# Linear attention with a feed-forward layer: other durations in the planner, and an order number of its own for every unit and step

## The chip, the cores and the metric

The kernel runs on one core of a Trainium2 chip. The metric is the device time of one execution in microseconds. Three runs of the kernel before the change took 551.27, 548.26 and 547.93 us; the median is 548.26 us.

## The reference

There are 4 batches, 8 heads, 768 positions and 48 values per head. An attention with a decaying state per head is followed by a feed-forward layer of width 2048 with squared ReLU over all 3072 tokens, in float32.

```python
for t in range(S):
    kt, vt, rt, wt = (k[:, :, t], v[:, :, t], r[:, :, t], w[:, :, t])
    cur = np.einsum('bhd,bhe->bhde', u[None] * kt, vt)
    y[:, :, t] = np.einsum('bhd,bhde->bhe', rt, state + cur)
    state = wt[:, :, :, None] * state + np.einsum('bhd,bhe->bhde', kt, vt)
x = np.ascontiguousarray(y.transpose(0, 2, 1, 3)).reshape(B * S, H * D)
h = np.maximum(x @ w_in, 0.0)
return h * h @ w_out
```

## The kernel before

The sequence is cut into 6 chunks of 128 positions. A chunk of one batch is a unit (24 units). For a unit, `attention(c, b, rank)` issues these steps: loads of r, k, w (`load`, two batches at a time) and of v (`v`); in chunk 0 transposes on TensorE (`turn`, L479), later a block transpose on DVE (`z`, L442) with 16 small transfers that spread it (`pt`, L452); the running products of the decay on DVE (`scan`, L491); their inverse through logarithm and exponential on ACT (`ln`, L498 and L499); scaled receptances (`rt`, L502) and keys (`kn`, L508, L509, L514) on DVE; the products with u on POOL (`rk`, L521 and L523) and their sums on DVE (`beta`, L527 to L530); the diagonals of the score matrices on ACT (`diag`, L541); a test of the value range on ACT (`far`, L543 and L544); the scores on TensorE (`mt`, L554); masks on DVE (`mask`, L557); then on TensorE the product with the state and the transposed keys (`ktp`, L576 and L581), after a copy on ACT (`kt`, L600) the product with the values and the outer product for the new state (`mix`, L589 and L608; in chunk 0 with a selection product L616 and a copy L620); the result x in a high and a low part on ACT and DVE (`x` and `x3`, L650 and L651), part of it moved by transfers (`send`, L658); and the state update on DVE and POOL (`S`, L670 and L673).

The feed-forward layer takes the 2048 hidden values in 16 blocks of 128, for each chunk. `ffn` issues per block nine hidden products (`hp`, L693) into one of two PSUM banks, the squared ReLU and its split in a high and a low part (`g`, L698 to L702, alternately ACT and DVE, three buffers), and per batch three output products (`ob`, L708) that add up in one of four banks. After the last block the banks are copied and stored (`os`, L715 to L719). The first 6 blocks of chunk 0 and all 16 of chunk 1 are done in two halves of two batches (256 columns instead of 512). The weights come in 8 groups (`load_w`), each split into a high and a low part on ACT, DVE and POOL (`split_w`, L393 to L414).

No instruction is issued by `attention` or `ffn` directly. Each call of `P.add` records a step with its engine, a planned duration, an order number (`rank`), and what it reads and writes. `Plan.order` then plays the whole program through with these durations: of the steps whose inputs are there, an engine takes the one that can start first, and among those the one with the lowest number. In the resulting order the instructions are emitted, so every engine has a fixed queue. The planned durations, the delays between engines (`LAT`), the queue times of transfers (`QUEUES`, `START`, `SLACK`) and the time to change TensorE between the whole array and its parts (`SWITCH`) act only through this order. In the first 110 us by the planner's own clock, it also fills gaps that it foresees on TensorE with throw-away transposes (fillers, L749): the gap less 0.3 us, divided by 0.12 us. The class `Ranks` gives the order numbers by formulas: an offset per step name, and per chunk, batch, weight group or feed-forward block a base.

[...]

## Time and profile before

| | |
|---|---|
| median of the runs | 548.26 us |
| span of the profiled execution | 546.8 us |
| matmul busy (PE) | 525.6 us, 96% |
| DVE, ACT, POOL busy | 368.9, 284.4, 101.8 us |
| idle time on PE, from the start to the first hidden product at 42.70 us | 7.66 us |
| from there to the first full-width hidden product at 83.20 us | 3.15 us |
| from there to the last matmul at 540.30 us | 3.92 us |
| the end, after it | 6.50 us |

The profile gives for the profiled execution its span, from the first to the last instruction, and no other time of it. PE is TensorE's matmuls, PEld its weight loads, DVE VectorE, ACT ScalarE, POOL GpSimd, SP the queue that issues most transfers. A row of the timeline has start and length in us, engine, line, operation, output and inputs, the number of instructions, and in brackets the idle time of the engine just before, with what ended it.

### The profile page before, as it was taken

How to read it: one execution, taken by the hardware profiler on the slowest of the kernel's cores; microseconds unless marked ns; L12 is line 12 of the kernel's file. 1: busy time of each engine (PE TensorE's matmuls, PEld its weight loads, DVE VectorE, ACT ScalarE, POOL GpSimd, SP SyncE). 2: the span in 40 equal slices, each digit the busy share in tenths (PEclk: the TensorE clock that was granted, in tenths of full speed). 3: DMA queues.
4: the chain of work that ended last, by engine and by line, in shares of the span. 5: the costliest groups of instructions: out<-in, count | busy, mean ns of one | idle time of the engine just before them, and what ended most of it. 6: DMA issues, size and time to landing. Idle time of an engine off the chain costs nothing.

```text
span 546.8 us, 12903 instructions
## 1 busy us (share of the span) xinstructions
PE 525.6 (96%) x5033; PEld 465.9 (85%) x5033; DVE 368.9 (67%) x770; ACT 284.4 (52%) x730; POOL 101.8 (19%) x121
## 2 busy tenths in 40 slices
PE   7889899999999998999999999999999999999995
PEld 6778798888899988988788887988888998998995
DVE  6979988998869676978869686886543423423322
ACT  3858586576664837475464747455343322432322
POOL 5234545152303102031303021020000000000000
PEclk9989999999999998999999999999999999999999
DMA  9989969447566575656546646633001000010001
GB/s 161 195 227 239 230 131 253 74 69 137 105 115 120 92 148 97 127 99 121 107 83 118 123 82 129 148 68 65 1 16 63 11 1 2 21 38 0 1 0 63
DMA packets 222979, 53.02 MB, mean 97 GB/s; under 512 B 212672, under 2 KB 217792, under 8 KB 222912
## 3 DMA queue, kind: packets, MB, share of 16 engines
q1 hardware_dynamic: 220016, 50.75, 46.7%
q10 hardware_dynamic: 2896, 1.38, 1.1%
q8 instruction: 42, 0.69, 0.6%
q14 instruction: 25, 0.20, 0.1%
HBM read 31.65 MB, written 4.72 MB: 67 GB/s over the span
## 4 chain that ended last, share of the span: by engine, by line
PE 40%; DVE 6%; SPq 2%; issue 1%; DMA 1%; ACT 1%; ACTq 0%; DVEq 0%
PE ob L708 19%; PE hp L693 18%; SPq L452 2%; DVE st L442 1%; PE a L589 1%; PE a L576 1%; DMA st<-in_r_dram 1%; DVE m L557 1%; PE a L554 1%; DVE pt L514 1%; DVE g L702 1%; DVE pt L491 0%; DVE m L509 0%; DMA v<-in_v_dram 0%; DVE pt L508 0%
## 5 line engine op out<-in xcount | busy, mean ns | idle before, releaser
L708 PE MATMUL ob<-wo,g 128*128 128x384 f32 x1152 | 224.0, 341 | 0.0
L693 PE MATMUL hp<-x,wi 128*128 128x512 f32 (+1 forms) x1062 | 220.0, 355 | 1.1 <-DVE g L702 1.0
L708 PEld LDWEIGHTS ob<-wo,g 128*128 128x128 f32 x1152 | 198.8, 188 | 5.2 <-issue 0.5
L693 PEld LDWEIGHTS hp<-x,wi 128*128 128x128 f32 x1062 | 175.2, 189 | 28.9 <-DVE g L702 2.8
L699 DVE SCALAR_TENSOR_TENSOR hp<-hp,t 128x512 f32<-128x512 f32 (+1 forms) x118 | 70.1, 594 | 83.4 <-ACT t L698 82.5
L698 ACT ACTIVATE t<-hp 128x512 f32<-128x512 f32 (+1 forms) x118 | 61.1, 518 | 107.3 <-PE ob L708 87.2
L702 DVE TENSOR_TENSOR g<-hp,g 128x512 fp32r<-128x512 f32 (+1 forms) x118 | 68.8, 583 | 34.7 <-ACT g L701 34.0
L701 ACT CAST g<-hp 128x512 fp32r<-128x512 f32 (+1 forms) x118 | 59.6, 505 | 58.2 <-DVE hp L699 58.1
L541 ACT ACTIVATE m<-diag,beta 128x64 f32<-128x64 f32 x192 | 50.7, 342 | 25.1 <-DVE beta L529 23.5
L521 POOL TENSOR_TENSOR st<-st 128x384 f32<-128x384 f32 x24 | 25.7, 1071 | 62.7 <-DVE st L442 60.6
L491 DVE TENSOR_TENSOR_SCAN pt<-pt,zero 112x128 f32<-112x128 f32 x80 | 30.1, 411 | 0.3 <-DMA pt<-st 0.2
L442 DVE STREAM_TRANSPOSE st<-st 128x1152 f32<-128x1152 f32 x20 | 27.2, 1363 | 4.2 <-DMA st<-in_r_dram 4.2
L554 PEld LDWEIGHTS a<-pt 48*64 48x64 f32 x768 | 19.1, 134 | 11.4 <-issue 3.2
L651 DVE SCALAR_TENSOR_TENSOR x<-a,x 112x128 fp32r<-112x128 f32 (+2 forms) x68 | 20.4, 329 | 11.2 <-ACT x L650 10.9
L557 DVE COPY_PREDICATED m<-caus,a 128x384 f32<-128x384 uint8 x48 | 26.3, 582 | 1.8 <-PE a L554 1.6
L554 PE MATMUL a<-pt 48*64 48x128 f32 (+1 forms) x768 | 22.6, 252 | 5.0 <-DVE pt L514 3.1
L589 PEld LDWEIGHTS a<-m,v 64*48 64x48 f32 (+1 forms) x768 | 20.2, 127 | 7.3 <-issue 3.2
L650 ACT ACTIVATE x<-a 112x128 fp32r<-112x128 f32 (+2 forms) x68 | 18.2, 316 | 15.6 <-PE a L608 7.6
L523 POOL TENSOR_TENSOR st<-st,un 128x384 f32<-128x384 f32 x24 | 24.9, 1040 | 1.4
L589 PE MATMUL a<-m,v 64*48 64x64 f32 (+3 forms) x768 | 24.3, 250 | 0.6 <-ACT nothing L640 0.5
L673 POOL TENSOR_TENSOR S<-S,Ec 112x192 f32<-112x192 f32 x16 | 9.4, 589 | 76.0 <-DVE S L670 71.2
L498 ACT ACTIVATE m<-pt 112x512 f32<-112x512 f32 x24 | 15.1, 633 | 15.5 <-DVE pt L491 15.3
(86 smaller groups left out, 441.7 us busy)
## 6 DMA issues: line engine op xcount, KB each, us to landing
pt<-st SPq DMA_DIRECT2D x120, 96.0 KB, 2.3
ro<-in_moe_w_out_dram SPq DMA_DIRECT2D x8, 768.0 KB, 6.9
v<-in_v_dram SPq DMA_DIRECT2D x88, 48.0 KB, 2.5
st<-in_w_dram SPq DMA_DIRECT2D x11, 384.0 KB, 4.0
st<-in_k_dram SPq DMA_DIRECT2D x11, 384.0 KB, 5.1
st<-in_r_dram SPq DMA_DIRECT2D x11, 384.0 KB, 6.1
out_dram<-q SPq DMA_DIRECT2D x20, 192.0 KB, 1.9
ri<-in_moe_w_in_dram SPq DMA_DIRECT2D x8, 384.0 KB, 6.5
```

Of the source, the lines that this page charges most:

```text
L442: V.transpose(out=zt[:, i].rearrange("a t p q i -> a t (p q) i"), in_=sv[:, :, i].rearrange("s t p q x -> s t (p q) x"))
L491: lambda p=p: V.tensor_tensor_scan(out=pt[:, 0, p], data0=src(0)[:, p], data1=zero.broadcast_to([HP, C]), initial=1.0, op0=ALU.mult, op1=A ...
L541: A.activation(Ms[j].tile[:, mo(p, y):mo(p, y) + Q], diag2, AF.Copy, scale=beta.tile[:, i:i + 1])
L554: T.matmul(mts[j].tile[q * Q:q * Q + Q, o:o + C - y * Q], kq[js, g:g + Q], pt[js, 1, 2 * q + p, y * Q:], start=True, stop=True, skip_group ...
L557: P.add("dve", 0.53, rank("mask"), lambda j=j: V.copy_predicated(out=mv(Ms[j]), mask=caus.broadcast_to([128, 2, W]), data=mv(mts[j])), r=[ ...
L589: T.matmul(spot(p)[to:to + n + D, y * Q:], vt.tile[qs, o - n:o + D], Ms[j].tile[qs, mo(p, y):mo(p, y) + C - y * Q], start=(c == 0 and p == ...
L693: T.matmul(hp.tile[:, 0:n], wi[f][:, wl, kt], xT[:, kt, xl, xs], start=(m == 0), stop=(m == 3 * KT - 1))
L698: P.add("act", 0.5 if full else 0.28, rank("g"), lambda: A.activation(t(), h(), AF.Relu), r=[hp], w=[(g, 1)])
L699: P.add("dve", 0.61 if full else 0.33, rank("g"), lambda: V.scalar_tensor_tensor(out=h(), in0=h(), scalar=0.0, in1=t(), op0=ALU.max, op1=A ...
L701: P.add("act", 0.53 if full else 0.31, rank("g"), lambda: A.copy(out=hi(), in_=h()), r=[hp], w=[(g, 0)])
L702: P.add("dve", 0.61 if full else 0.33, rank("g"), lambda: V.tensor_tensor(out=lo(), in0=h(), in1=hi().bitcast(F32), op=ALU.subtract), r=[h ...
L708: T.matmul(obs[b][:, 0:DM], g.tile[0][:, gl, o:o + C], wo[f][:, wl], start=(f == 0 and m == 0), stop=(f == NF - 1 and m == 2))
```

## The change

The planner gets other figures throughout: delays between engines, the first transfer's delay (`START` 2.4 to 3.6), the margin after a transfer (`SLACK` 2.0 to 1.0), three times instead of one for changing TensorE's mode, an issue time for each transfer instead of one per queue, and other durations for nearly all steps. [...] The tiles for v are taken in unit order from chunk 1 on. The order numbers come from tables: one per unit and step name (`UNITS`, 24 rows of 23), one per weight group (`LOAD`, `SPLIT`), one per feed-forward block and step name (`FFN`). What is computed, and with which instructions, stays; the number of fillers goes from 169 to 183. All line numbers behind the class `Ranks` grow by 139.

```diff
-    LAT = {"pe": 0.24, "act": 0.14, "dve": 0.14, "pool": 0.15}
-    QUEUES = {"sp": 0.5, "actq": 0.36}
-    LANES, RUNS, SLACK, START = 8, 2300, 2.0, 2.4
-    SWITCH, KEEP = 0.094, 1.0
+    LAT = {"pe": 0.22, "act": 0.13, "dve": 0.11, "pool": 0.13}
+    QUEUES = ("sp", "actq")
+    LANES, RUNS, SLACK, START = 8, 2300, 1.0, 3.6
+    ENTER, LEAVE, BETWEEN, KEEP = 0.147, 0.2, 0.09, 1.0
...
-                free[unit] = at + self.QUEUES[s.engine]
+                free[unit] = at + s.issue
...
-                        free[unit] += self.SWITCH
+                        free[unit] += self.ENTER if not mode else self.BETWEEN if s.mode else self.LEAVE
...
-    U0 = (-83, -59.75, 60, 76.25)
-    OFF = {'hp': 147.75, 'g': 6.75, 'ob': 70, 'os': 85.75}
-    LAG = 80
+    UNITS = (
+        (-1354.91, -1161.61, 40.98, -392.53, -1448.01, 172.35, -3.19, -1499.94, -1249.87, 191.9, -1500, 1014.93, -6.91, -1480, 150.66, 35.23, 145.22, -1468.33, 0, 0, 0, 0, 0),
...
+    FFN = {
+        (0, 1.0): (1232.86, 185.26, -86.32, 0),
...
-        return 32 * (c - 1) + 8 * b - 4 + self.AT[name]
+        return self.UNITS[4 * c + b][self.NAMES.index(name)]
...
-        vt = Slot("v" if c else "v0")
+        vt = Slot("v", 4 * c + b) if c else Slot("v0")
...
-                P.add("pe", 0.5, rank("turn"), turn, r=[(st, ui, i)], w=[ps[i]])
+                P.add("pe", 0.36, rank("turn"), turn, r=[(st, ui, i)], w=[ps[i]])
...
-        P.add("dve", 0.75, rank("beta"), sums, r=[(st, ui, 1)], w=[beta])
+        P.add("dve", 1.04, rank("beta"), sums, r=[(st, ui, 1)], w=[beta], port=True)
...
-        P.add("pe", 0.95, rank("mt"), scores, r=RK + KK, w=mts, mode=1, claim=Ms)
+        P.add("pe", 0.69, rank("mt"), scores, r=RK + KK, w=mts, mode=1, claim=Ms)
...
-            P.add("dve", 0.53, rank("mask"), lambda j=j: V.copy_predicated(out=mv(Ms[j]), mask=caus.broadcast_to([128, 2, W]), data=mv(mts[j])), r=[mts[j]], w=[Ms[j]])
+            P.add("dve", 0.47, rank("mask"), lambda j=j: V.copy_predicated(out=mv(Ms[j]), mask=caus.broadcast_to([128, 2, W]), data=mv(mts[j])), r=[mts[j]], w=[Ms[j]])
...
-        P.add("pe", 2.1 if full else 1.1, rank("hp"), first, r=wkeys("wi") + [x for b in range(*bs) for x in xkeys(c, b)], w=[hp])
+        P.add("pe", 2.075 if full else 1.07, rank("hp"), first, r=wkeys("wi") + [x for b in range(*bs) for x in xkeys(c, b)], w=[hp])
...
-            P.add("pe", 0.525, rank("ob"), second, r=wkeys("wo") + [(g, 0), (g, 1)], w=[("ob", b)])
+            P.add("pe", 0.52, rank("ob"), second, r=wkeys("wo") + [(g, 0), (g, 1)], w=[("ob", b)])
```

Three places of the order show what moves. The first is ACT's queue in chunk 0, from the step that begins the split of the second group of `w_out` (`ro_62`) to the x of the second unit (`x_136`); `m` with `diag` are diagonals, `m_158<-a` the copies of the second unit's transposed keys. Before:

```order
L393 ACTIVATE q_150<-ro_62 128x768
L541 ACTIVATE m_159<-diag_125,beta_170 128x64 x4
L600 COPY m_158<-a_147 128x224
L600 COPY m_158<-a_148 128x224
L541 ACTIVATE m_161<-diag_125,beta_170 128x64 x4
L541 ACTIVATE m_160<-diag_125,beta_171 128x64 x4
L466 DMA v_94<-in_v_dram 64x4x48 x2
L650 ACTIVATE x_136<-a_147 128x2x128
L650 ACTIVATE x_136<-a_148 128x128
```

And now:

```order
L532 ACTIVATE q_150<-ro_62 128x768
L680 ACTIVATE m_159<-diag_125,beta_171 128x64 x4
L680 ACTIVATE m_161<-diag_125,beta_171 128x64 x4
L789 ACTIVATE x_136<-a_147 128x2x128
L789 ACTIVATE x_136<-a_148 128x128
L739 COPY m_158<-a_147 128x224
L739 COPY m_158<-a_148 128x224
```

The x of the second unit stands after two groups of diagonals instead of three, and ahead of the copies instead of behind them.

The second is DVE's queue where the last two units of chunk 0 get their keys: `pt_130<-a` (L514, now L653) is the key product that the scores of such a unit wait for, `beta` are the sums of a unit of chunk 1 (before), `S` is a state update, `hp` and `g` belong to the feed-forward layer. Before:

```order
L670 TENSOR_TENSOR S_133<-a_148,Ec_166 112x96
L527 TENSOR_REDUCE beta_168<-st_151 128x8
L528 TENSOR_TENSOR beta_168<-beta_168 64x4
L529 TENSOR_TENSOR beta_168<-beta_168 64x4
L530 TENSOR_TENSOR beta_168<-beta_168 64x4
L514 TENSOR_TENSOR pt_130<-a_147,m_157 112x2x4x64
L702 TENSOR_TENSOR g_97<-hp_146,g_97 128x256
```

And now, around both key products of this pair:

```order
L809 TENSOR_TENSOR S_132<-a_148,Ec_165 112x96
L648 SCALAR_TENSOR_TENSOR m_156<-pt_130,m_156 112x512
L653 TENSOR_TENSOR pt_130<-a_147,m_157 112x2x4x64
L838 SCALAR_TENSOR_TENSOR hp_146<-hp_146,t_96 128x256
L653 TENSOR_TENSOR pt_130<-a_148,m_156 112x2x4x64
L841 TENSOR_TENSOR g_95<-hp_146,g_95 128x256
```

The sums of the unit of chunk 1 (L527 to L530) stand directly ahead of a key product before; now none do.

The third is TensorE's queue in chunk 1, at the unit of batch 0 (state `S_131`): the last scores (`a<-pt`, L554, now L693) and the first products with the state (L576, now L715). Before:

```order
L554 MATMUL a_148<-pt_129 64x64
L708 MATMUL ob_142<-wo_71,g_97 128x384 x3
L693 MATMUL hp_145<-x_136,wi_77 128x512 x9
L576 MATMUL a_147<-pt_129,S_131 64x128
L576 MATMUL a_147<-pt_129,S_131 48x128
```

And now:

```order
L693 MATMUL a_147<-pt_129 64x64
L693 MATMUL a_148<-pt_129 64x64
L715 MATMUL a_147<-pt_129,S_131 64x128
L715 MATMUL a_147<-pt_129,S_131 48x128
L715 MATMUL a_148<-pt_129,S_131 48x128
```

An output and a hidden product stood between the scores and the state product of this unit; now nothing does.

More of the change, by code (lines that the diff above doesn't have):

```diff
@@ L55, in pool, with add @@
         self.pools[name] = [[0.0, t] for t in tiles]
-    def add(self, engine, cost, rank, fn, r=(), w=(), after=(), runs=128, port=False, mode=0, claim=(), more=0):
+    def add(self, engine, cost, rank, fn, r=(), w=(), after=(), runs=128, port=False, mode=0, claim=(), more=0, issue=0.5):
         s = Step()
+        s.issue = issue
         s.mode, s.more, s.fill = mode, more, (0, None)
@@ L196 @@
-    AT1 = {'load': -67.5, 'z': 222.75, 'pt': -247.25, 'rk': 205.25, 'beta': 122.75, 'far': 121, 'v': -0.25, 'scan': 54, 'ln': 129.25, 'rt': -164.5, 'kn': -179, 'diag': 307, 'mt': -111.75, 'mask': -258.5, 'ktp': -150.5, 'kt': -29, 'mix': -182.5, 'x': 282, 'x3': -277.75, 'send': -154.5, 'dS': 325, 'S': -15.75}
-    U0 = (-83, -59.75, 60, 76.25)
-    C1 = (-17.75, 54, 74.25, 163.25)
-    W0 = (-263.75, -87.25, -59.25, -20.75, 22.25, 4.5, 110.5, 165.5)
-    WL = (-93.5, -123, -116.25, -63, -46.75, -41.25, -197.5, -176.25)
@@ L201 @@
-    OFF = {'hp': 147.75, 'g': 6.75, 'ob': 70, 'os': 85.75}
-    LAG = 80
-    def unit(self, c, b, name):
-        if c == 0:
-            return self.U0[b] + self.AT0[name]
-        if c == 1:
-            return self.C1[b] + self.AT1[name]
-        return 32 * (c - 1) + 8 * b - 4 + self.AT[name]
+    NAMES = ('load', 'v', 'turn', 'scan', 'ln', 'rt', 'kn', 'rk', 'beta', 'diag', 'far', 'mt', 'mask', 'mix', 'kt', 'x', 'dS', 'S', 'z', 'pt', 'ktp', 'x3', 'send')
+    UNITS = (
[24 rows of a table added]
+    )
+    LOAD = (-1273.71, -900.27, -547.16, -422.59, 579.46, 579.24, 858.31, 1017.12)
@@ L379, in load_w @@
             n = (2 * R, D, D, D, D)[i]
-            P.add("sp", 0.0059 * n if i < KT else 0.5, rank, lambda to=to, src=src: nc.sync.dma_start(out=to, in_=src),
-                  w=[("wi", g, i)], after=before, runs=n)
-        P.add("sp", 2.4, rank, lambda: nc.sync.dma_start(out=wo_r[g], in_=w_out32[g]), w=[("wo", g, 0, 0)],
-              after=before, runs=256)
+            P.add("sp", (1.45, 0.72, 0.72, 0.47, 0.47)[i], rank, lambda to=to, src=src: nc.sync.dma_start(out=to, in_=src),
+                  w=[("wi", g, i)], after=before, runs=n, issue=0.48)
+        P.add("sp", 2.7, rank, lambda: nc.sync.dma_start(out=wo_r[g], in_=w_out32[g]), w=[("wo", g, 0, 0)],
+              after=before, runs=256, issue=0.5)
     def split_w(g, rank):
@@ L434, in load @@
                                           in_=src[b0:b0 + m, :, ss, :].rearrange("b h s d -> s (b h) d"))
-                    P.add("sp", 1.05 * m, rank("load") + b0 - b, load, w=[(st, x, i) for x in range(b0 - b, b0 - b + m)], after=after, runs=128 * H * m)
+                    P.add("sp", 0.25 + 0.94 * m, rank("load") + b0 - b, load, w=[(st, x, i) for x in range(b0 - b, b0 - b + m)], after=after, runs=128 * H * m, issue=0.6)
             if c > 0:
@@ L599, in evacuate @@
             for i, t in enumerate(both_yb):
-                P.add("act", 0.3, rank("kt"), lambda i=i, t=t: A.copy(out=kv(Kt, i * 2 * HP, None), in_=kv(t, 2 * C, None)), r=[(t, "kt")], w=[(Kt, i)])
+                P.add("act", 0.24, rank("kt"), lambda i=i, t=t: A.copy(out=kv(Kt, i * 2 * HP, None), in_=kv(t, 2 * C, None)), r=[(t, "kt")], w=[(Kt, i)])
         def outer():
```

220 lines of the change are left out of this document (169 added, 51 removed), and 23 rows, old and new, of the table UNITS.

## The prediction

> **What bounds the kernel now.** I read the page first: its busy rows and the chain that ended last say that TensorE (PE) sets the end and that DVE, ACT and POOL do not.
>
> ```profile
> span 546.8 us, 12903 instructions
> PE 525.6 (96%) x5033; PEld 465.9 (85%) x5033; DVE 368.9 (67%) x770; ACT 284.4 (52%) x730; POOL 101.8 (19%) x121
> PE 40%; DVE 6%; SPq 2%; issue 1%; DMA 1%; ACT 1%; ACTq 0%; DVEq 0%
> ```
>
> Then the busy time by stretch, cut where the program changes its kind of work: up to the first hidden-layer product (42.7), to the first full-width one (83.2), through the attention of the later chunks, and the end. Behind the span stand the busy times of PE (x matmuls), the granted PE clock, the DMA share and GB/s.
>
> ```profile
> 0.00:42.70 42.70, 35.04 (x396) 0.96 0.99 194
> 42.70:83.20 40.50, 37.35 (x417) 1.00 0.94 199
> 83.20:180.00 96.80, 96.18 (x1065) 1.00 0.63 125
> 180.00:270.00 90.00, 87.70 (x1083) 0.98 0.59 112
> 270.00:540.30 270.30, 269.30 (x2079) 1.00 0.25 51
> 540.30:546.80 6.50, 0.02 (x1) 0.89 0.35 122
> ```
>
> PE stands idle 42.70 - 35.04 = 7.66 us, then 3.15, 0.62, 2.30 and 1.00: 14.7 us before the last matmul. The 6.50 at the end are the copy and store of the last outputs. The change leaves every matmul of the computation in place, so what it can win is this idle time, slow-clock time, and fillers, the throw-away transposes that the planner puts into gaps it foresees during the first 110 us of its own reckoning. The program has 169 fillers before and 183 after. Where they stand matters more than how many there are.
>
> **The first stretch.** The columns of the next rows are start, length, engine, line, operation, count and, in brackets, idle time before it.
>
> ```profile
> 12.12 2.67 PE L749 MATMUL a<-ident 128*128 128x128 f32 x23
> 36.52 0.93 ACT L393 ACTIVATE q<-ro 128x768 f32<-128x768 f32 x1 [1.69 <-DMA ro<-in_moe_w_out_dram]
> 37.34 0.82 ACT L541 ACTIVATE m<-diag,beta 128x64 f32<-128x64 f32 x3
> 38.30 0.57 ACT L600 COPY m<-a 128x224 f32<-128x224 f32 x2
> 38.76 2.03 ACT L541 ACTIVATE m<-diag,beta 128x64 f32<-128x64 f32 x8
> 40.69 0.54 ACT L650 ACTIVATE x<-a 128x256 fp32r<-128x256 f32 x2
> 37.08 5.07 PE L749 MATMUL hp<-ident 128*128 128x128 f32 x31
> 42.08 0.68 PE L608 MATMUL a<-v,m 64*64 64x48 f32 x32
> 42.69 1.34 PE L693 MATMUL hp<-x,wi 128*128 128x256 f32 x9
> ```
>
> A filler takes 2.67 / 23 = 0.116 us at the full clock. The first hidden product at 42.69 waits for two things: the x of the second unit (batch 1), which ACT writes at 40.69, and the outer product of that unit (L608), which stands ahead of it on PE behind 31 fillers. Both come after ACT's wait for a weight load that lands at 36.52. The order of ACT from that load on is the first place shown with the change: one group of four diagonals (L541) and the issue of two loads leave the way to x, and x moves ahead of the copies. The loads on SP's queue keep their order as far as this weight group, so I keep its landing. After: 36.52 + 0.82 (step to the next) + 1.93 (eight diagonals, 38.76 to 40.69) + 0.54 (x) + 0.57 (copies) = 40.4, outer product 0.61 and a hand-over, first hidden product at 41.4: 1.3 us earlier. Against it stands the first unit. The mask of its second half moves on DVE behind the second unit's key product and sums and two steps of a weight split, the fillers ahead of its first value product grow from 13 to 37 (24 x 0.116 = 2.8 us), and its copies on ACT fall behind the logarithms of the next pair, so PE reaches the second unit's scores some 3 us later. That just about uses up the wait for the load. If it runs over, the cover is gone and the 29 extra fillers ahead of the first hidden product (143 before, 172 after) are paid: 29 x 0.116 = 3.4 us. Bounds -1.3 to +3.4; I take 0, since both chains meet within a microsecond.
>
> **The second stretch (42.7 to 83.2).** PE interleaves the last two units of chunk 0 with half-width hidden products.
>
> ```profile
> 58.48 1.64 DVE L528 TENSOR_TENSOR beta<-beta 64x4 f32<-64x4 f32 x1
> 60.15 0.91 DVE L529 TENSOR_TENSOR beta<-beta 64x4 f32<-64x4 f32 x1
> 61.91 0.90 PE L554 MATMUL a<-pt 48*64 48x128 f32 x32 [2.03 <-DVE pt L514]
> 64.50 0.88 PE L749 MATMUL hp<-ident 128*128 128x128 f32 x6
> 68.84 1.36 PE L749 MATMUL hp<-ident 128*128 128x128 f32 x11
> 73.63 0.82 PE L749 MATMUL a<-ident 128*128 128x128 f32 x6
> ```
>
> The longest stall, 2.03 us, is PE waiting for the last key product (L514) of a unit. That stood on DVE behind the sums of a unit of the next chunk, two of whose tiny steps took 1.64 and 0.91 us. In the new order (second place) both key products of this pair stand close behind one another with no sums ahead of them, so this stall has no cause left. Fillers in this stretch fall from 26 to 11: 15 x 0.116 = 1.7 us. Of the 3.15 us idle I do not take all: each of the three filler groups that remain leaves at least the 0.3 us that the planner's rule subtracts, so 1.1 us in all, and I allow one short stall of 0.74 (the row at 270.33 below): 3.15 - 1.84 = 1.3. Together -3.0, bounds -4.9 (all of it) to 0 (each stall comes back elsewhere).
>
> **The third stretch (83.2 to 540.3).** Three stalls are left here, and one costs more than its length. The last four rows are single microseconds; behind the span: PE, PEld, DVE, ACT and POOL busy (x instructions), then clock, DMA share and GB/s.
>
> ```profile
> 146.97 1.34 PE L693 MATMUL hp<-x,wi 128*128 128x256 f32 x9 [0.54 <-DVE g L702]
> 206.63 1.60 PE L554 MATMUL a<-pt 48*64 48x128 f32 x32 [1.89 <-DVE S L670]
> 270.33 1.03 PE L576 MATMUL a<-pt,S 48*64 48x128 f32 x16 [0.74 <-DVE m L557]
> 207.00:208.00 1.00, 1.00 (x31) 1.00 (x30) 0.97 (x2) 0.00 (x0) 1.00 (x3) 0.69 0.91 156
> 208.00:209.00 1.00, 1.00 (x11) 0.88 (x7) 0.93 (x4) 0.22 (x1) 0.54 (x1) 0.50 0.82 143
> 209.00:210.00 1.00, 1.00 (x6) 1.00 (x5) 1.00 (x3) 1.00 (x5) 0.00 (x0) 0.50 0.72 124
> 210.00:211.00 1.00, 1.00 (x7) 0.99 (x6) 1.00 (x3) 1.00 (x5) 0.00 (x0) 0.60 0.48 79
> ```
>
> After the 1.89 us stall the granted clock is 0.69, 0.50, 0.50 and 0.60 for four microseconds: 0.31 + 0.50 + 0.50 + 0.40 = 1.7 us of work not done. Without the three stalls the stretch gains 0.54 + 1.89 + 0.74 + 1.7 = 4.9 us.
>
> [...]
>
> The order also brings a new stall. In the third place shown, the state product (L576, now L715) of batch 0 in chunk 1 follows its own scores directly. It waits for the two masks on these scores, and where an output and a hidden product stood between, no matmul covers them now.
>
> ```profile
> 28.85 0.90 PE L554 MATMUL a<-pt 48*64 48x128 f32 x32
> 29.80 1.07 DVE L557 COPY_PREDICATED m<-caus,a 128x384 f32<-128x384 uint8 x2 [0.15 <-PE a L554]
> 30.92 0.55 PE L589 MATMUL a<-m,v 64*48 64x128 f32 x8
> ```
>
> There PE's scores end at 29.75 and the product behind the masks starts at 30.92: 1.2 us with DVE free. It is the only such pair of a unit. Elsewhere the spacing of scores, copies and buffers looks much like before, with a few half-width products closer together; I allow 0.8 for those, about the row at 270.33 once more. Together -4.9 + 1.2 + 0.8 = -2.9. Bounds: -4.9, and +2.0 if the new stall cools PE (1.2 + 1.7) and four more of the size of the row at 146.97 come with it (2.2) while only that row, the 270.33 one and the tail of the cooling (3.1) go.
>
> **Small terms.** One change of PE between whole and split array drops out (76 to 75 each way). A first output product behind such a group takes 0.72 instead of 0.52.
>
> ```profile
> 379.22 0.52 PE ob L708 x3
> 420.22 0.72 PE ob L708 x3
> ```
>
> That is -0.2. The end is alike: 36 output matmuls stand behind the last hidden product, still far more than its evacuation needs, and the last bank's copy and store follow as before: 0. The planned durations themselves run nowhere; they act only through the order.
>
> **Sum.** 0 - 3.0 - 2.9 - 0.2 = -6.1 us against the span of 546.8, so 540.7; the median of the runs, 548.26, lies 1.46 above that span, and with the same distance I get 542.2. The ends of the bounds: -1.3 - 4.9 - 4.9 - 0.2 = -11.3, so 537.0; +3.4 + 0 + 2.0 = +5.4, so 553.7.
>
> **Rivals.** *The stalls only move.* For it: PE is 96% busy and 14.7 us idle, and every earlier gap had been planned away as well, by a reckoning the chip did not keep to; the orders of all engines are new, so new misfits appear at random. Gain of half the second stretch, nothing in the third: 1.5 - 0.2 less, 546.6, range 544.7 to 549.5. Chance 0.30.
>
> *Late start, slower than before.* Place: the first unit's mask and copies pushed back on DVE and ACT. From the point where PE ends the second unit's value products later than 39.3 (36.52 + 0.82 + 1.93), each further microsecond delays all that follows. Price: 3.4 us of fillers plus a slow clock of 1.7 us if PE waits about 1.9 us there, with the second stretch's gain lost, since its weights arrive at the same times: 548.26 + 5.1 = 553.4, range 549.5 to 554.5. Against it: the hand chain meets the load within a microsecond. Chance 0.09.
>
> *All of it.* The start 1.3 earlier and hardly a stall left: 538, range 536.5 to 539.3. For it: all three long stalls lose their cause. Against: the uncovered mask pair. Chance 0.14.
>
> That the order stays as it was is excluded: it differs on all engines. The forecast case, 539.3 to 544.7, has 0.47.
>
> **Chances.** One per cent, about what a measurement of this kernel can tell from no change, is 5.5 us: 542.8 and 553.7. Faster: 0.14 and two thirds of the forecast case, 0.46. Slower: half of the late start, 0.05, and 0.01 for the unforeseen. Within: 0.48. The range from 537.0 to 549.5 leaves out the late start, half of "all of it" and a little of the rest.
>
> **What would show it.** Right: the first hidden product within 41 to 43.5; the first full-width one at 80 us or earlier; no wait of PE on L653 above 1 us; from there to the last matmul below 3 us of PE idle, a wait of about 1.2 us of L715 on the mask near 110 us, no microsecond at half clock. Wrong: a first hidden product after 45, or waits of PE on DVE in the third stretch that add up to more than 4 us.

## The result, and the profile after

The changed kernel takes 545.03 us (median of 5 runs, 544.59 to 545.76), the kernel before 548.26 (median of 5, 547.80 to 551.27): a ratio of 0.9943 with a 95% interval from 0.9918 to 0.9967. Two more sets of runs later gave 545.30 against 548.10 (0.9938, 0.9916 to 0.9960) and 545.26 against 547.46 (0.9958, 0.9943 to 0.9973). So it gains 0.4 to 0.6%, some 2.2 to 3.2 us. One execution of the kernel before in the second of these sets, of 1859.57 us, counts in no ratio. The forecast was 542.2; the number lies inside the range, and inside "within 1%".

The profiled execution took 545.76 us with a span of 543.9, 0.7 above its median. The busy row of its page:

```profile
PE 526.4 (97%) x5047; PEld 465.7 (86%) x5047; DVE 367.1 (67%) x770; ACT 281.8 (52%) x730; POOL 101.4 (19%) x121
```

The busy time cut at the same events as before (first hidden product, first full-width one, last matmul); behind the length of each stretch stand PE, PEld, DVE, ACT and POOL busy (x instructions), clock, DMA share and GB/s:

```profile
0.00:41.42 41.42, 36.39 (x424) 33.18 (x424) 33.38 (x84) 23.79 (x66) 18.49 (x35) 1.00 0.95 174
41.42:80.62 39.20, 35.89 (x397) 32.52 (x395) 34.99 (x67) 26.32 (x64) 20.22 (x12) 1.00 0.93 219
80.62:180.00 99.38, 98.05 (x1085) 86.83 (x1085) 88.09 (x188) 65.67 (x181) 29.60 (x29) 1.00 0.63 128
180.00:270.00 90.00, 88.45 (x956) 79.21 (x957) 67.20 (x153) 50.49 (x144) 16.43 (x23) 1.00 0.57 107
270.00:537.60 267.60, 267.59 (x2192) 233.92 (x2190) 143.43 (x281) 114.67 (x278) 16.63 (x22) 1.00 0.27 53
537.60:543.90 6.30, 0.02 (x1) 0.00 (x0) 0.00 (x0) 0.83 (x2) 0.00 (x0) 0.67 0.28 99
```

The first stretch is shorter by 42.69 - 41.42 = 1.3 us, the second by 40.48 - 39.20 = 1.3, and the third (80.6 to 537.6) is as long as before, 457.0 against 457.2. From 7.27 us, where the record of the clock begins, to the last matmul the clock is full; before, two windows in that part were at half rate. PE's largest waits, as total, times and longest:

```profile
PE hp L832 <- DVE g L841: 3.2, 5, 1.1
PE a L693 <- DVE pt L653: 1.4, 1, 1.4
```

The first fillers and then the longer stalls one by one on PE's timeline, with the first hidden and the first full-width product (start, length, idle time in brackets):

```profile
1.60 4.95 PE L888 MATMUL a<-ident 128*128 128x128 f32 x22 [1.60 <-POOL ident masks.py:199]
16.08 0.90 PE L693 MATMUL a<-pt 48*64 48x128 f32 x32 [1.40 <-DVE pt L653]
41.42 1.34 PE L832 MATMUL hp<-x,wi 128*128 128x256 f32 x9
74.20 1.34 PE L832 MATMUL hp<-x,wi 128*128 128x256 f32 x9 [1.02 <-DVE g L841]
79.81 0.98 PE L847 MATMUL ob<-wo,g 128*128 128x384 f32 x4 [1.36 <-DVE g L841]
80.62 3.61 PE L832 MATMUL hp<-x,wi 128*128 128x512 f32 x15
114.00 1.12 PE L715 MATMUL a<-pt,S 48*64 48x128 f32 x16 [0.69 <-DVE m L696]
189.49 1.34 PE L832 MATMUL hp<-x,wi 128*128 128x256 f32 x9 [1.12 <-DVE g L841]
```

The first row shows what the clock column leaves out. Its 22 fillers take 4.95 / 22 = 0.225 us each, about twice the 0.116 of a filler at full clock, though the column prints 1.00 there. The record of the clock begins with the first full grant (7.27 us here, 6.00 in the profile of before, 4.99 with four stalls covered, 11.48 without fillers). In the profiles of before and after, the transposes ahead of that point start 213 ns apart, those behind it 109. So up to there TensorE runs at about half its rate, in both kernels. Windows at half clock are counted below from that first grant on.

Before, PE's longest waits were for key products, a state (L670) and masks. Now the half-width hidden blocks wait for their own evacuation: the last step of it, the subtraction L841 on DVE that fills `g`. What stood ahead of it on DVE's timeline:

```profile
77.75 1.67 DVE L669 TENSOR_TENSOR beta<-beta 64x4 f32<-64x4 f32 x1
79.35 0.41 DVE L841 TENSOR_TENSOR g<-hp,g 128x256 fp32r<-128x256 f32 x1
187.75 1.37 DVE L630 TENSOR_TENSOR_SCAN pt<-pt,zero 112x128 f32<-112x128 f32 x4 [1.65 <-DMA st<-in_w_dram]
189.04 0.40 DVE L841 TENSOR_TENSOR g<-hp,g 128x256 fp32r<-128x256 f32 x1
```

And on POOL's, at the first of these places:

```profile
77.56 1.84 POOL L553 TENSOR_TENSOR wo<-q,wo 128x768 fp32r<-128x768 f32 x1 [1.84 <-ACT wo L552]
```

At 79.35 the subtraction stands behind one 64x4 step that took 1.67 us, beginning 0.19 us after a POOL product and ending with it; in 21 of its 24 executions in this trace the same step takes 0.15. At 189.04 it stands behind four scans whose transfer landed late: DVE waited 1.65 us at the head of its queue. So the planner's new figures did not keep either from happening: the sums now carry `port=True`, with which the planner keeps a step from running beside POOL's in its own reckoning, and on the chip POOL's product still ran beside them. Why the step took 1.67 us beside that product was not tested.

### The profile page after: what moved, and what is told of

Read it like the earlier page. It is cut to its first block, busy times and chain, and to the rows that moved or that the text cites. A ratio compares the mean times of both kernels' runs of the same rounds, so it can differ in the third digit from the quotient of the medians.

```text
span 543.9 us, 12917 instructions
## 1 busy us (share of the span) xinstructions
PE 526.4 (97%) x5047; PEld 465.7 (86%) x5047; DVE 367.1 (67%) x770; ACT 281.8 (52%) x730; POOL 101.4 (19%) x121
## 4 chain that ended last, share of the span: by engine, by line
PE 77%; DMA 10%; DVE 4%; ACT 3%; SPq 3%; issue 1%; POOL 0%; ACTq 0%; DVEq 0%
PE hp L832 33%; PE ob L847 32%; DMA ri<-in_moe_w_in_dram 4%; DMA v<-in_v_dram 3%; PE a L693 3%; PE a L728 3%; DMA st<-in_w_dram 2%; PE a L715 2%; SPq L572 2%; PE a L720 1%; PE a L747 1%; ACT m L680 1%; SPq L605 1%; DVE g L841 1%; DVE pt L630 1%
## 5 line engine op out<-in xcount | busy, mean ns | idle before, releaser
L832 PEld LDWEIGHTS hp<-x,wi 128*128 128x128 f32 x1062 | 173.1, 188 | 32.8 <-DVE g L841 6.8
L841 DVE TENSOR_TENSOR g<-hp,g 128x512 fp32r<-128x512 f32 (+1 forms) x118 | 68.9, 585 | 32.3 <-ACT g L840 31.6
L660 POOL TENSOR_TENSOR st<-st 128x384 f32<-128x384 f32 x24 | 24.3, 1017 | 65.6 <-DVE st L581 58.4
L630 DVE TENSOR_TENSOR_SCAN pt<-pt,zero 112x128 f32<-112x128 f32 x80 | 29.0, 412 | 1.7 <-DMA st<-in_w_dram 1.7
L790 DVE SCALAR_TENSOR_TENSOR x<-a,x 112x128 fp32r<-112x128 f32 (+2 forms) x68 | 20.2, 329 | 12.2 <-ACT x L789 10.9
L662 POOL TENSOR_TENSOR st<-st,un 128x384 f32<-128x384 f32 x24 | 27.3, 1141 | 1.6
L693 PEld LDWEIGHTS a<-pt 48*64 48x64 f32 x768 | 19.2, 133 | 7.8 <-ACT m L680 1.6
L693 PE MATMUL a<-pt 48*64 48x128 f32 (+1 forms) x768 | 22.8, 250 | 1.4 <-DVE pt L653 1.4
L812 POOL TENSOR_TENSOR S<-S,Ec 112x192 f32<-112x192 f32 x16 | 8.1, 508 | 82.8 <-DVE S L809 82.8
```

The source lines that it names most:

```text
L630: lambda p=p: V.tensor_tensor_scan(out=pt[:, 0, p], data0=src(0)[:, p], data1=zero.broadcast_to([HP, C]), initial=1.0, op0=ALU.mult, op1=A ...
L662: P.add("pool", 0.97, rank("rk"), lambda: G.tensor_tensor(out=rk(), in0=rk(), in1=un.rearrange("s (h d) -> s h d", d=D), op=ALU.mult), w=[ ...
L693: T.matmul(mts[j].tile[q * Q:q * Q + Q, o:o + C - y * Q], kq[js, g:g + Q], pt[js, 1, 2 * q + p, y * Q:], start=True, stop=True, skip_group ...
L832: T.matmul(hp.tile[:, 0:n], wi[f][:, wl, kt], xT[:, kt, xl, xs], start=(m == 0), stop=(m == 3 * KT - 1))
L841: P.add("dve", 0.6 if full else 0.33, rank("g"), lambda: V.tensor_tensor(out=lo(), in0=h(), in1=hi().bitcast(F32), op=ALU.subtract), r=[hp ...
```

## The experiments

**Eleven runs followed**, of eight new kernels and of the two old ones, in three sets. Each set ran on another chip, with its own runs of the kernel before beside it; the changed kernel ran beside the second and the third. The two kernels with inserted stalls were executed once each and stand further down. The lengths of the three stretches in each profile, worked out from the starts of the first hidden and first full-width product and the end of the last output matmul, with the windows of 3.41 us at half clock that lie in each:

| kernel | median us | before beside it | first | second | third | half-clock windows |
|---|---|---|---|---|---|---|
| before | 548.26 | | 42.7 | 40.5 | 457.2 | 1, 0, 1 |
| before again | 548.88 (one) | 548.10 | 42.7 | 41.3 | 456.7 | 1, 1, 1 |
| before, three stalls covered | 545.98 | 548.10 | 41.3 | 40.6 | 456.2 | 1, 0, 0 |
| before, four covered | 546.81 | 547.46 | 42.6 | 40.6 | 456.1 | none |
| after | 545.03 | 548.26 | 41.4 | 39.2 | 457.0 | none |
| after again | 545.30 | 548.10 | 40.9 | 39.5 | 457.8 | none |
| after, third | 545.26 | 547.46 | 41.1 | 39.2 | 457.1 | none |
| four moves | 545.07 | 547.38 | 40.4 | 37.9 | 458.1 | none |
| more moves | 548.69 | 548.10 | 42.3 | 38.7 | 461.0 | 1, 0, 0 |
| no fillers | 549.17 | 547.38 | 46.1 | 40.4 | 456.4 | ten from 14.9 to 49.0, 1 at 86.6 |
| times only | 557.31 | 547.38 | 43.2 | 40.0 | 466.0 | 0, 1, 3 |

The kernel before took 544.8 to 550.0 us in the first set alone, with mean granted clocks from 0.999 down to 0.985; the changed one stayed between 544.0 and 546.1 in all sets.

**The durations without the order numbers.**

```diff
-    LAT = {"pe": 0.24, "act": 0.14, "dve": 0.14, "pool": 0.15}
+    LAT = {"pe": 0.22, "act": 0.13, "dve": 0.11, "pool": 0.13}
...
-        P.add("pe", 0.95, rank("mt"), scores, r=RK + KK, w=mts, mode=1, claim=Ms)
+        P.add("pe", 0.69, rank("mt"), scores, r=RK + KK, w=mts, mode=1, claim=Ms)
```

> The changed planner's durations, issue times and mode-change times, but every step's order number from the formulas of before. Theory 1 (the order numbers carry the change; the durations only tell the planner when a buffer is free): no gain, 547.5 to 552, and the first hidden product is not at 41.4 us. Theory 2 (truer durations alone carry it): within 1 us of the changed kernel's 545.0, with the first hidden product near 41.4 and the first full-width block near 80.6.

557.31 us against 547.38 (ratio 1.0174, 1.0143 to 1.0206), worse than either theory had it. The largest group of PE's waits:

```profile
PE hp L694 <- DVE g L703: 8.3, 6, 4.2
```

The longest of these on PE's timeline, and two of the split steps on DVE's ahead of L703:

```profile
120.06 2.50 PE L694 MATMUL hp<-x,wi 128*128 128x512 f32 x5 [4.18 <-DVE g L703]
114.96 2.77 DVE L398 TENSOR_SCALAR q<-q 128x768 uint32<-128x768 uint32 x2
118.26 1.15 DVE L402 SCALAR_TENSOR_TENSOR q<-ri,q 128x768 uint32<-128x768 uint32 x1
```

The new durations alone cost ten microseconds: under the formulas they bring DVE's weight-split steps ahead of an evacuation for which PE then waits 4.18 us. With these durations, then, the gain needs the new order numbers. Whether the tables would win with the old figures is open: with only the delays or only the transfer margin put back, the planner reaches a point where no step may go next, so the tables belong to these exact figures.

**No fillers.**

```diff
-    P.filler = lambda bank: T.transpose(out=bank[:, 0:128], in_=ident, identity=ident)
```

> The changed kernel without any of its 183 filler transposes (172 of them before the first hidden product); the output is the same. Theory 1 (fillers only fill waits and keep the clock up): the first hidden product stays within 0.5 us of 41.4, the granted clock is below full for some us around it, and the time is 546.5 to 550. Theory 2 (fillers hold steps up that stand behind them): the first hidden product at 40.4 or earlier, 543 to 544.5.

549.17 us (ratio 1.0030, 1.0009 to 1.0050 against before), and so, by the ratios to before, 4 to 5 us above the changed kernel (1.0030 / 0.9958 and 1.0030 / 0.9938). Busy time and clock by stretch:

```profile
15.00:30.00 15.00, 8.73 (x82) 7.29 (x83) 11.65 (x22) 10.47 (x29) 3.75 (x3) 0.50 1.17 181
30.00:49.00 19.00, 14.35 (x161) 12.29 (x160) 15.20 (x34) 10.56 (x34) 6.71 (x7) 0.50 0.85 220
```

Without fillers the start runs 34 us at half clock, and the first hidden product comes at 46.1 instead of 41.4. The time is in the range of theory 1, but neither theory had the rest: the first product moves, and later. The start's steps wait for one another across engines, so slow matmuls may lengthen the chain; that is an argument, not a measurement. The fillers are worth 4 to 5 us here, and the half clock comes where they are missing, but how much of the 4 to 5 us is the clock's is not shown. Of the ten executions, one with a recorded mean clock of 0.973 took 547.71 us and one with 0.997 took 549.68; as the record leaves out the beginning, 0.997 need not mean a full clock there.

**Four stalls taken away by moving steps in the planned list.** The numbers are steps in the order of their creation; each pair puts the first behind the second.

```diff
+    MOVES = ((277, 398), (273, 398), (272, 398), (576, 390), (575, 389), (1068, 832), (1067, 832), (1066, 832), (1065, 832), (454, 542), (453, 542))
+
     def run(self):
-        for s in self.order():
+        out = self.order()
+        for n, m in self.MOVES if self.filler else ():
+            i = next(i for i, s in enumerate(out) if s.n == n)
+            j = next(i for i, s in enumerate(out) if s.n == m)
...
+            out.insert(j, out.pop(i))
+        for s in out:
```

> The changed kernel with its planned list altered at four places, each where a stall of TensorE was seen: at 74 us two steps of the weight splits (L536 to L545, with the copy L552 between them) go behind g L841; at 79.8 us the four sums of beta and the first half of the diagonals go behind the next hidden block's relu product L838 and copy L840; at 189.5 us four scans L630 that wait for a transfer go behind g L841; at 114 us two output products L847 go behind the scores L693, so that they run while the masks L696 are written. Theory 1 (these stalls are waits for an engine's queue and nothing else is late behind them): 1.02 + 1.36 + 1.12 + 0.69 us go but for some tenths, 540.8 to 542.2, with no wait of TensorE over 0.5 us at these places. Theory 2 (the third stretch is bound by something late behind each stall, so a stall moves on to the next block): 543.5 to 545.2, with new waits of like length within 10 us behind the places.

545.07 us (0.9967, 0.9948 to 0.9986 against before): nothing won against the changed kernel, whose ratios were 0.9938 to 0.9958. Its second stretch is 1.3 to 1.6 us shorter, as hoped (37.9 against 39.2 to 39.5), and the third 0.3 to 1.1 longer. In this kernel all lines are 11 further on: L858 is the output product, L848, L851 and L852 the evacuation, L691 the diagonals, L563 a split's copy. PE's timeline:

```profile
86.45 1.86 PE L858 MATMUL ob<-wo,g 128*128 128x384 f32 x7 [1.20 <-ACT g L851]
190.79 1.33 PE L843 MATMUL hp<-x,wi 128*128 128x256 f32 x9 [1.02 <-DVE g L852]
```

ACT's, ahead of the first of them:

```profile
84.15 1.05 ACT L691 ACTIVATE m<-diag,beta 128x64 f32<-128x64 f32 x4
85.10 0.82 ACT L563 CAST wi<-q 128x768 fp32r<-128x768 f32 x1
85.82 0.57 ACT L851 CAST g<-hp 128x512 fp32r<-128x512 f32 x1
```

The view by windows there (PE, PEld, DVE, ACT, POOL busy, as above):

```profile
82.00:86.00 4.00, 3.25 (x20) 2.90 (x18) 4.00 (x6) 4.00 (x14) 0.00 (x1) 1.00 0.82 190
```

PE reaches the first full-width block 2.0 to 2.3 us earlier, and waits 1.20 us at the next evacuation, which now stands in ACT's queue behind the work that had been put off. From 82 to 86 DVE and ACT are both busy all of the time. Theory 2 holds at this place, and its range of time as well. At 189 us the four scans are behind the evacuation now, and a stall of nearly the same length (1.02 for 1.12) stands at the next block: the scans, and what follows from them on DVE, are ahead of that block's evacuation instead. Only the mask pair gave a little (0.43 for 0.69).

**What took their place moved as well.**

```diff
-    MOVES = ((277, 398), (273, 398), (272, 398), (576, 390), ...
+    MOVES = ((274, 376), (273, 376), (277, 377), (272, 375), (576, 390), (575, 389), (579, 402), (538, 402), (260, 405), (259, 405), (254, 403), (539, 404), (255, 404), ...
```

> The four moves once more, with what took the place of the stalls moved as well: at 72 to 75 us the weight-split steps go behind the next L838 too; at 82 to 86 us the diagonals L680, the second pass L683 of the far test and the splits L540, L545 and L552 of the next group go behind the evacuation (L837 to L841) of the first full-width hidden block, and at 188 us a scan L630, L647 and L638 behind that of its half-width block. Theory 1 (each stall is a matter of what stands ahead of the evacuation in ScalarE's and VectorE's queues): the 0.71, 1.20 and 1.02 us that the four moves left go but for some tenths, 542 to 543.5. Theory 2 (ScalarE and VectorE are behind with their whole work there, so the wait comes back at the next block or at the next user of what was put off): 544.3 to 545.3.

548.69 us, 3.4 above the changed kernel beside it and level with the kernel before (1.0013, 0.9993 to 1.0033). Its third stretch is the longest of all with these tables. PE's timeline:

```profile
79.77 1.43 PE L858 MATMUL ob<-wo,g 128*128 128x384 f32 x6 [2.02 <-ACT g L851]
90.75 1.88 PE L843 MATMUL hp<-x,wi 128*128 128x512 f32 x7 [0.58 <-POOL wi L564]
```

DVE's, ahead of the first stall:

```profile
76.09 2.48 DVE L556 SCALAR_TENSOR_TENSOR q<-ro,q 128x768 uint32<-128x768 uint32 x1
```

The stalls are back and larger: one split step took 2.48 us beside a POOL product (0.95 for another step of the same line at 73.58), and 10 us on, PE waits for the weights themselves (POOL's L564), for the splits that had been put off. That is the mechanism of theory 2, at a price it did not have: 544.3 to 545.3 was expected. A wait taken from PE at one place is paid at another here. But "behind with their whole work" is true for a few microseconds only: from 70 to 90 us DVE is busy 17.1 us and ACT 14.8 in the kernel with four moves, 18.0 and 14.0 in this one. So it is not shown that no order would fit.

**A ladder of stalls.** In the last chunk, where PE has no stalls, one is put behind the output products of seven hidden blocks:

```diff
+                for _ in range({1: 1, 3: 2, 5: 3, 7: 4, 9: 5, 11: 6, 13: 3}.get(f, 0) if c == NC - 1 and b == B - 1 else 0):
+                    if not _:
+                        T.transpose(out=pas[0][:, 0:128], in_=ident, identity=ident)
+                        t = P.pools["m"][0][1]
+                    V.tensor_copy(out=t[:, 0:384], in_=pas[0][:, 0:384])
+                else:
...
+                        T.transpose(out=pas[0][:, 0:128], in_=t[:, 0:128], identity=ident)
```

> The changed kernel with stalls of TensorE put into the last chunk, where it has none: behind the output products of hidden blocks 1, 3, 5, 7, 9, 11 and 13 a transpose, then 1, 2, 3, 4, 5, 6 and 3 copies of 128x384 on VectorE that read it, then a transpose that reads the copy. The stalls should be near 0.9, 1.4, 2.0, 2.5, 3.1, 3.6 and 2.0 us (0.54 us a copy and some 0.4 us to and from), 15.5 us in all. Theory 1 (as in the profile of before at 207 to 211 us: 1.89 us of waiting is answered by half the clock for some 3 us): the stalls from about 1.9 us up are each followed by one to three us of reduced clock, each with about 1.7 us more than the stall; time near 569. [...]

568.67 us in one execution, near the 569 of theory 1, and yet not as it had it. The five longer stalls on PE's timeline, in order:

```profile
508.50 0.33 PE L855 MATMUL a<-ident,m 128*128 128x128 f32 x1 [1.83 <-DVE m L852]
520.25 0.47 PE L855 MATMUL a<-ident,m 128*128 128x128 f32 x1 [2.42 <-DVE m L852]
531.39 0.33 PE L855 MATMUL a<-ident,m 128*128 128x128 f32 x1 [3.02 <-DVE m L852]
546.90 0.33 PE L855 MATMUL a<-ident,m 128*128 128x128 f32 x1 [3.61 <-DVE m L852]
555.97 0.33 PE L855 MATMUL a<-ident,m 128*128 128x128 f32 x1 [1.84 <-DVE m L852]
```

Two shorter ones (0.65 and 1.24 us) come before them and were not answered. Of these five, those of 1.83, 2.42 and 3.61 us were, that of 3.02 and the last, of 1.84, were not. The granted clock in the trace falls at 509.73, 519.97 and 547.27 and rises 3.413 us later each time; the falls are 3 and 8 times 3.413 us apart. So the clock seemed to be set once for each window of a grid. The 3.02 us stall lies across a border of that grid, at 530.21, with 1.84 us before it and 1.18 behind. Two experiments follow from that.

**Seven equal stalls**, the same edit with four copies at each place.

> Seven stalls of the same length in the last chunk of the changed kernel, behind the same seven hidden blocks as in the ladder, each of four copies (2.42 us in the ladder). Theory 1 (a window of 3.41 us of a free grid is answered by half clock in the next one if TensorE idles over about 1.84 us of it): some of the seven are answered and some not, and which ones follows from the grid: those with over 1.85 us inside one window, three to six of them; each answered one costs some 1.5 us; time near 569 to 573. Theory 2 (the length decides): all seven are answered, near 574, or none, near 563.

570.08 us in one execution. All seven stalls are 2.42 or 2.43 us long; three were answered. The view by windows, cut on the grid that the first fall (511.05) fixes:

```profile
507.64:511.05 3.41, 0.98 (x7) 0.65 (x6) 2.75 (x5) 0.60 (x1) 0.00 (x0) 1.00 0.00 0
511.05:514.46 3.41, 3.41 (x10) 2.64 (x9) 0.78 (x2) 0.58 (x1) 0.00 (x0) 0.50 0.02 5
521.29:524.70 3.41, 2.37 (x14) 2.37 (x15) 3.32 (x6) 1.18 (x2) 0.00 (x0) 1.00 0.00 0
528.12:531.53 3.41, 0.98 (x7) 0.69 (x6) 2.42 (x6) 0.59 (x1) 0.00 (x0) 1.00 0.00 0
531.53:534.94 3.41, 3.41 (x9) 2.73 (x10) 0.49 (x1) 0.00 (x0) 0.00 (x0) 0.50 0.00 0
545.18:548.60 3.42, 1.22 (x8) 1.22 (x8) 2.66 (x6) 0.89 (x2) 0.00 (x0) 1.00 0.02 5
555.42:558.84 3.42, 1.80 (x11) 1.81 (x12) 2.09 (x4) 0.00 (x0) 0.00 (x0) 1.00 0.00 0
```

Where PE was busy 0.98, 0.98 or 1.22 us of a window, the next window is at half clock for the whole of its 3.41 us and PE then does 9 or 10 matmuls in it; where the border cut the stall and 1.80 to 2.37 us were left busy, the clock stayed. That is theory 1: it is the share of a window, not the length of the stall.

**The kernel before, once more.**

> The kernel before once more, for its profile. Theory 1 (the clock is granted or halved for whole windows of 3.41 us of a grid that runs free of the program; a stall is answered where it fills more than about half of one window): stalls at the same places, within 0.3 us of their length, but reduced clock at other ones of them, and always for 3.41 us; each such window is worth 1.2 to 1.7 us. Theory 2 (a stall of given length is always answered alike): reduced clock behind the same two stalls, at 36 to 40 and 207 to 211 us.

548.88 us in one execution. Of the stalls at 34.88, 61.91 and 206.63 us in the first profile of before, the first is not there, the last is 2.29 us long in place of 1.89 and answered again, and that of 61.91, not answered then, now is. Two windows of the first profile of before, cut on its own grid:

```profile
57.21:60.62 3.41, 2.67 (x20) 2.35 (x19) 3.34 (x7) 1.39 (x3) 3.34 (x3) 1.00 1.01 281
60.62:64.03 3.41, 2.12 (x40) 1.80 (x40) 3.38 (x9) 2.93 (x10) 0.43 (x1) 1.00 1.09 214
```

And the wait on PE's timeline in the second profile:

```profile
62.13 1.13 PE L554 MATMUL a<-pt 48*64 48x128 f32 x20 [2.05 <-DVE pt L514]
```

The view by windows there:

```profile
58.70:62.12 3.42, 1.39 (x11) 1.07 (x9) 3.35 (x5) 1.06 (x5) 2.57 (x2) 1.00 1.05 269
62.12:65.53 3.41, 3.40 (x38) 3.15 (x38) 2.88 (x6) 3.38 (x11) 0.00 (x0) 0.50 1.05 249
```

The same wait of the same instruction, 2.03 and 2.05 us, fell across a border in one run, with 0.74 and 1.29 us of idle on its two sides, and inside a window in the other, with 2.03. So the grid of theory 1 holds on this stall of the kernel's own. "More than about half" of a window does not hold everywhere: the windows ahead of the low grants at 36.72 us (first profile) and 31.40 us (second) had 1.51 and 1.50 us of idle, less than half of 3.41. The second stretch was 0.8 us longer for it.

**The kernel before with its stalls covered.** Fillers go ahead of the steps that wait, into a free bank, and the waits remain:

```diff
+    MORE = {78: 11, 158: 14, 1121: 13}
+
     def run(self):
         for s in self.order():
             for _ in range(s.fill[0] if self.filler else 0):
                 self.filler(s.fill[1])
+            for _ in range(self.MORE.get(s.n, 0) if self.filler else 0):
+                self.filler(s.free)
```

> The kernel before with fillers added in front of three of its steps, where its profile shows the longest stalls outside the start: 11 ahead of the selection of L616 (1.51 us at 34.88), 14 ahead of the scores at 61.91 (2.03 us) and 13 ahead of the scores at 206.63 (1.89 us). The stalls themselves stay. Theory 1 (what the change took away is mostly reduced clock that follows such stalls, not the stalls): no reduced clock from 30 to 215 us, and a median of 544.8 to 546, within 1 us of the changed kernel. Theory 2 (the change gained by its order): the median stays within 0.7 us of the kernel before.

545.98 us against 548.10 (0.9952, 0.9932 to 0.9972), 0.7 above the changed kernel beside it. No reduced clock between 21 and 540 us. Theory 1 as far as its number goes: 38 fillers in the kernel before win 2.1 us. In its start, though, a stall of 2.41 us at 17.27 was answered.

**That one covered too** (14 more fillers ahead of the first scores).

> The kernel before with the fillers of the run with three covered stalls and 14 more ahead of the first scores (15.91 us in the profile of before, with 1.12 us of waiting there; 2.41 us at 17.27 in the profile of that run, with the clock halved from 17.7 to 21.1). Theory 1 (the clock was the whole of the gain, and the rest of it stood in the start): 544.9 to 545.6, within 0.4 us of the changed kernel in the same rounds. Theory 2 (about 0.7 us of the gain came from the order): 545.7 to 546.3, 0.5 to 1 us above the changed kernel.

546.81 us against 547.46 (0.9986, 0.9969 to 1.0003), and 1.5 above the changed kernel beside it. From the first full grant, at 4.99 us, the profile has no reduced clock up to the last matmul:

```profile
0.00:42.64 42.64, 35.76 (x421) 31.54 (x421) 32.50 (x84) 24.49 (x68) 16.98 (x35) 1.00 1.04 191
42.64:83.23 40.59, 38.87 (x430) 36.05 (x429) 37.90 (x72) 30.02 (x79) 20.55 (x12) 1.00 0.96 201
```

So theory 1 falls in its strong form: with the clock full from there on, the kernel before is still some 1.5 us behind. Covering the start's stall won nothing that shows: the start ended at 42.6, and at 41.3 in the profile with the stall and its half-clock window. What the covers are worth is 2.1 us in one set and 0.65 in the other, and the difference between the sets is as large as the question. The share of the clock in the gain is therefore some 0.6 to 2 us.

The single executions bear on that difference between the sets, since each has its recorded mean clock beside its time. In the second set the kernel before had 0.9916 on average and the changed one 0.9978; a straight line through the executions of the kernel before has 302 us per unit of clock, so the distance stands for 1.9 us. In the third set the figures are 0.9942, 0.9979 and 173 us, which makes 0.6 us. In the same way the covers should have won 1.9 and 0.5, and they won 2.1 and 0.65. These are estimates: the lines fit loosely (correlations of -0.70 and -0.47), and a low clock comes with long waits, which they count as well. By them, the kernel before met fewer half-clock windows in the third set, and 0.9 to 1.6 us of the gain are left for the order.

**The changed kernel, twice more.**

> The changed kernel once more, timed with the others. Both theories: median 544.6 to 545.8. Theory 1 (of the grid): none or one reduced window before 535 us, since no stall behind the start is over 1.4 us. For its start: first hidden product between 40.4 and 41.5 us if the microsecond by which two profiles of the same start differ is chance.

> The changed kernel once more, to be compared with the run before with covered stalls in the same rounds: 544.6 to 545.8 by either theory, with no reduced clock between 45 and 535 us.

545.30 and 545.26 us, as expected. Its first hidden product came at 41.4, 40.9 and 41.1 in three profiles. The four kernels made from it that keep its fillers have the same program up to there, and came to 40.4 (four moves), 42.3 (more moves, with a half-clock window at 17.7), 41.0 and 40.8 (inserted stalls). So one and the same start differs by 2 us between profiles. None of the three profiles of the changed kernel has a half-clock window behind the first grant and before the last matmul.

## Why the prediction was right, and where it was not

**The number** fell in the range, 3 us above the forecast. It lies just outside the forecast's own case (539.3 to 544.7) and inside that of the rival "the stalls only move" (544.7 to 549.5), which is also most of what happened, with one difference: the start gained. That it fell in the range is in part luck: the range takes in this rival whole, and the start came out 1.3 to 1.9 us better than forecast, the second stretch 1.7 and the third 2.7 worse.

**Start: 0 forecast, -1.3 to -1.9 measured.** The hand chain gave 41.4 and the profile has 41.42, but not by that chain. ACT's step on the awaited load, and the diagonals behind it, in the profile after and then in that of four moves, whose start is the same program:

```profile
35.83 0.93 ACT L532 ACTIVATE q<-ro 128x768 f32<-128x768 f32 x1
37.40 2.02 ACT L680 ACTIVATE m<-diag,beta 128x64 f32<-128x64 f32 x8 [0.65 <-DVE beta L668]
35.40 0.92 ACT L543 ACTIVATE q<-ro 128x768 f32<-128x768 f32 x1 [0.47 <-DMA ro<-in_moe_w_out_dram]
```

In the profile after, the step on the load began 0.69 us before the 36.52 that the sum kept, without waiting for the transfer. The diagonals then waited 0.65 us for sums on DVE, which stand behind the masks of scores that PE ended at 33.80, and began at 37.40 for 37.34 in the sum. From there on the terms were right (x at 39.33 for 39.27). So the agreement to 0.02 us is luck: an earlier load and a wait that the chain did not have made up for each other. In the profile of four moves ACT did wait for the load; it landed at 35.40, and the first hidden product came at 40.4. The steps that failed are the landing kept at 36.52 and the choice of 0 between the two chains. The second unit's last value products on PE's timeline:

```profile
38.40 0.88 PE L728 MATMUL a<-m,v 64*64 64x128 f32 x24
```

They end at 39.3, the very point from which the rival had the start late. It was not passed, and the 29 additional fillers did not make the start longer. With two chains this close, which one ends last differs from run to run.

**Second stretch: -3.0 forecast, -1.3 measured.** The named cause went as said: there is no wait on L653 in this stretch. (The sign "no wait of PE on L653 above 1 us" failed as written, by the 1.40 us at 16.08, in the start.) Fillers fell from 26 to 6 and not to 11, since five of the 11 that stand behind the first hidden product are in the third stretch. They gave 2.9 us for 1.7. But the idle time, forecast at 1.84, stayed at 3.31 (3.15 before): two new stalls, 1.02 and 1.36 us, at evacuations of half-width blocks. And PE's other work, which the sum took as unchanged, grew by 1.4 us: counted from start to start of the matmuls, the same 60 output products take 12.0 us for 11.1, the 64 value products 2.85 for 2.6, and scores, hidden products and transposes another 0.3. What makes them slower is not shown. So two steps failed: the allowance for one short stall of 0.74, and the products' own time, put at nothing. The first took the waits that PE had before for the list of what could be late, and did not ask what stands on DVE ahead of g L841. The first full-width product came at 80.62, not by 80.

**Third stretch: -2.9 forecast, -0.2 measured.** The stalls of 0.54, 1.89 and 0.74 went, and one of 1.12 came, at 189 us. The uncovered mask pair came where it was foreseen, 0.69 at 114 us for 1.2 near 110. PE was idle 2.9 us (below 3, as said; 3.3 and 3.1 in the other two profiles), and no microsecond ran at half clock. Yet the stretch is no shorter. The five fillers at 87 us cost 0.5. The half clock's price was about right (without idle time and fillers the two profiles of before take 453.2 and 452.7 us here, the two covered ones 451.6 and 451.7: 1.0 to 1.7 us for one window). The step that failed is that the sum took PE's own work as unchanged. What it missed is a loss: against the covered kernel before, with a full clock too and 456.1 to 456.2 us, the new order takes 457.0 to 457.8. Without idle time and fillers that is 451.6 and 451.7 against 453.6 to 454.0, 2 us and a little more, spread over scores (0.7), output products (0.7), full-width hidden products (0.4) and others, counted from start to start of PE's matmuls. Waits too short to be shown, and changes between kinds of work, are possible causes; none was shown.

**The clock term (1.7 us).** The row at 208 was read as the price of any stall of about 1.9 us. In the last chunk, with stalls inserted, what told the answered stalls from the others was not their length but the idle time within one window of 3.41 us: 2.14 or more was always answered, 1.62 or less never, 1.83 once and 1.84 twice not. The stall of 61.91 cost a half-clock window in one profile of the kernel before (2.03 us of idle in one window) and none in the other (0.74 and 1.29 in two); the one at 206.63 was answered in both. The term was taken whole for a stall that is answered often; a stretch without its window is 1.0 to 1.7 us shorter, as said above. What the bounds of the third stretch call cooling is the half clock of the rows at 207 to 211 us. The window behind 206.63 did go; the time was lost elsewhere.

**Small terms and tail.** Tail 6.3 for 6.5; the -0.2 for one mode change is below what the stretches resolve. Two sums are a little off: 0.54 + 0.74 + 1.7 is 3.0 for the 3.1 in the upper bound, and three times 0.3 is 0.9 for 1.1. Neither would move the forecast by more than 0.2 us.

**Rivals.** "Late start" did not occur. "All of it" had the start right. "The stalls only move" is borne out at the places where steps were moved in two runs; its time, 546.6, was 1.6 too high, since the start gained.

**What remains of the gain**: with full clocks on both sides, -1.5 in the start (42.6 to 41.1, though the other covered profile has 41.3, so that this share may be chance), -1.4 in the second stretch (40.6 to 39.2), about +1.0 in the third (456.1 to 457.1), and on top the half-clock windows that the kernel before meets in the third stretch, one between 207 and 212 us in both its profiles, 0.6 to 1.1 us of the stretch (457.2 and 456.7 for 456.1), and the changed one does not.

## What to carry to other kernels

A planned order that removes PE's stalls gains only as long as the engines behind it have time to spare: before moving a step, read what stands in DVE's and ACT's queues in the few microseconds around it, and not how busy they are over the span. In the kernel before, a wait of 2.03 to 2.05 us was followed by 3.41 us at half clock in one profile and not in the other, and its time varies more from run to run (544.8 to 550.0 us, against 544.0 to 546.1 after). A few dozen throw-away matmuls ahead of the waiting steps took 0.65 to 2.1 us off here with the waits left where they were. A hand chain that ends at the measured time is not yet a right one: look at what each of its steps waited for. Durations and order numbers that were found together belong together; half of this change was ten microseconds worse than none.

## What the hardware showed that was not expected

The low grants of the clock between the first full grant and the last matmul lasted 3.41 us or a multiple of it in these profiles, and within one execution they lie on one grid. In the profile of before they fall at 36.72 and 207.39 us, 50 times 3.413 apart; in before again at 62.12 and 208.89, 43 times; in the ladder 3 and 8 times, and in the equal stalls (511.05, 531.53, 548.60) 6 and 5 times. The grid of before again lies 1.5 us off that of before. In the last chunk, windows with 2.14 us of idle or more (ladder 2.14 and 3.04, equal stalls 2.20, 2.43 and 2.43) were followed by half clock, and those with 1.62 or less were not; of three in between, all in the ladder, the one with 1.83 was and two with 1.84 were not. In the start of before, 1.51 us of idle ahead of 36.72 was followed by half clock. Without fillers the clock was at half from 15 to 49 us, ten windows in a row, with 10.9 us of PE idle in these 34, some 1.1 a window on average. So something other than idle time alone seems to count; that was not tested.

The record of the granted clock begins with the first full grant. Up to there, 6.00 us into the profile of before and 7.27 into that of after, transposes start 213 ns apart, 109 behind it, while the profile prints a clock of 1.00.

A 64x4 step of DVE took 1.67 us in place of 0.15 (after, 77.75), and a 128x768 one 2.48 in place of 0.95 (more moves, 76.09), each beside a product of POOL (1.84 and 2.27 us).
